# The skip term of an SSM on GpSimd, and one slot for each kind of projection weights

## The chip, the cores and the metric

The kernel runs on one core of a Trainium2 chip. The metric is the device time of one execution, in microseconds (us). A core has a matrix engine (TensorE, PE in the profile), VectorE (DVE), ScalarE (ACT), GpSimd (POOL) and SyncE (SP). Each works through its own queue in order and waits for the others by semaphores. Here nearly all transfers are issued from SP's queue, in the order in which the program was written; if one of them has to wait, those behind it wait too. TensorE writes to PSUM, in eight banks of 128 x 512 f32; the other data is in SBUF.

## The reference

A state-space model (SSM) and an attention read the same x (2048 positions, 1024 features, bf16), and a gate mixes them for each position:

```
Bu   = x @ B_bar^T                      (complex, 1024 states)
h[t] = Lam_bar * h[t-1] + Bu[t]
a    = 2 * Re(h @ C^T) + x * Dskip
b    = softmax(q k^T / sqrt(32)) v @ wo     (32 heads of 32, q k v = x @ wqkv)
g    = sigmoid(sum(x * gate_w))
out  = g * a + (1 - g) * b
```

The change is in how `x * Dskip`, the skip term, gets into `g * a`.

## The kernel before

**Bursts.** The backbone is 512 bursts: 8 groups of 4 heads, 8 blocks of 256 queries in a group, 8 steps over the keys in a block. A burst (function `burst`, line 1612) issues eight score matmuls (L1624) into four PSUM banks, and two exponentials of 1024 columns on ACT (L1643). Three pairs of banks take turns, so the scores of a burst wait until the first exponential of the burst before is over. In 184 bursts DVE computes a quarter of the second exponential by a polynomial: one operation takes the scores out of PSUM (L1633), and ACT's shortened exponential (L1640, 768 columns) is ordered behind it; then three passes on DVE (L1667, L1668, L1664), and one on GpSimd (L1665, into the tile xp) for each pair of such bursts. TensorE multiplies the exponentials by V (L1709, and L1688 for those from xp). At the end of a block DVE normalizes (L1722, L1723), and a transposing transfer stores the result.

**Dense work.** All other matmuls are cut into chains that are laid between the bursts, four matmuls of 512 columns (or as many columns) to a burst. All chains of the loop in `build` (line 1734) accumulate in bank 7, one after the other, and each ends with an eviction by DVE:

- u chains (`d_u`, L1457, eviction L1461): x times B, 64 of them; the result goes to DRAM and comes back as items (load L1474), for which DVE does the rotation and the scan (`item_ops`, L1353 and L1362). The weights B come through a ring of three slots (L1076).
- projection chains (`d_qk` L1426, `d_v` L1445): K, V and Q of the next group, 12 for each group.
- C chains (`d_c`, line 1496): 32, each for 128 positions and 512 features: 16 matmuls of h with C (L1504), and four matmuls of 128 columns (L1510) with x and a diagonal matrix of Dskip, which add x * Dskip into the same bank. The eviction (L1517) multiplies by the gate into one f32 tile (Ag), and the tile is stored to DRAM (L1518).
- output chains (`d_out`, L1535): attention output times wo; their eviction (L1547) adds g * a, loaded again (L1527).

**Order.** `build` writes the program burst by burst, and picks the next chain by fixed rules: projections when the group's end comes near, else C chains, else u chains. A C chain may begin when the items of its chunk are done and C has been folded (`fold_ops`, 24 operations of DVE, queued when the last of C has been asked for). It counts a chain's weight in matmuls of 512 columns; the four small matmuls of a C chain have weight 0. From estimated times it decides between which chains the operations of DVE are put. In the 496 bursts of the loop there is dense work in every one, the last 4 with one matmul only.

**Memory.** K and V weights have two slots (groups in turn), Q weights one: `wq`, `wkv`. `ld_w` (line 1068) loads 256 KB; K and V of group g + 2 are asked for at burst 25 of group g, Q of group g + 1 at burst 28. C comes in 8 pairs of transposing loads (L1081), one pair every four bursts from burst 28 (`C_LOADS`). In the early bursts the tiles for C still hold exponentials (`plan`). wo comes in parts: rows 0 and 1 at burst 386 into slots of K and V, the rest after the last C chain, row 7 behind the last projection.

Of the kernel before, what the change touches and what calls it, by code (L numbers as in the profile page):

```python
# [6 lines left out]
BF = mybir.dt.bfloat16  # L7
# [925 lines left out]
C_LOADS = 28  # L933
# [25 lines left out]
class FastPath:  # L959

    def __init__(self, nc, S, es, d, flag):
# [17 lines left out]
        self.wo3 = [row(1024, 2), row(5120, 3), row(3072, 1), self.cT[0][:, 0:1, :], self.cT[0][:, 1:2, :]]  # L979
        self.wo = [(self.wo3[0][:, a, :], "wo0") for a in range(2)] + [(self.wo3[4][:, 0, :], "wo4")] + [(self.wo3[1][:, a, :], "wo1") for a in range(3)]  # L980
        self.wo += [(self.wo3[3][:, 0, :], "wo3"), (self.wo3[2][:, 0, :], "wo2")]
# [5 lines left out]
        self.hpx = wb[:, 5120:8192].rearrange("p (k n) -> p k n", k=6)  # L987
# [18 lines left out]
        self.diagD = T("diagD", [128, 8, 128], BF)  # L1006
# [58 lines left out]
    def w_of(self, g, part):  # L1065
        return (self.wkv[:, g % 2, part - 1], ("w", g % 2, part)) if part else (self.wq, ("w", 0, 0))
# [86 lines left out]
    def opening(self):  # L1153
# [10 lines left out]
        for word in self.OPENING.split():  # L1164
# [44 lines left out]
            elif op == "M":  # L1209
# [7 lines left out]
                self.diag_d()  # L1217
# [86 lines left out]
    def diag_d(self):  # L1304
        for j in range(8):
            self.pool(lambda e, j=j: e.tensor_scalar(self.diagD[:, j, :], self.ident[:], self.pf[:, 3, j:j + 1], 0.0, ALU.mult, ALU.add),
                      ["ident", ("pf", 3)], [("diagD", j)])
# [188 lines left out]
    def d_c(self, ch, tq, cb, k):  # L1496
# [11 lines left out]
        for q in range(4):  # L1508
            dt = 4 * cb + q
            mms.insert(5 * q + 3, (0, lambda e, f, l, q=q, dt=dt: e.matmul(ps[:, 7, 128 * q:128 * (q + 1)], xT[:, dt, 128 * tt:128 * (tt + 1)], self.diagD[:, dt, :],  # L1510
                                                                          start=False, stop=False), [("diagD", dt)] + self.xtok(ch)))
        a = self.Ag
        at = "Ag"
        tile = 2 * tt + cb

        def evac():
            self.dve(lambda e: e.tensor_scalar(a, ps[:, 7, :], self.gcol[:, 0, tt:tt + 1], None, ALU.mult), [("bank", 7), "g0"], [at], "evac_c")  # L1517
# [3 lines left out]
        return self.chain(mms, "c", evac)  # L1521
# [212 lines left out]
    def build(self):  # L1734
# [10 lines left out]
        for part in (1, 2):  # L1745
            self.ld_w(1, part)
# [38 lines left out]
        wo1 = wo6 = last = False  # L1785
# [4 lines left out]
        for p in range(first, NBURST):  # L1790
# [41 lines left out]
            if pg == 25 and g + 2 < GROUPS:  # L1832
                assert g or not (proj[0] or cur and cur.tag == "proj")
                for part in (1, 2):
                    self.ld_w(g + 2, part)
            if pg == 28 and g + 1 < GROUPS:
                assert not (cur and cur.tag == "proj")
# [4 lines left out]
            if not cs and cur is None and not wo1 and self.c_left[3] == 0:  # L1842
# [293 lines left out]
```

## Time and profile before

| | us |
|---|---|
| three runs | 927.49, 926.35, 927.41 |
| median | 927.41 |
| profiled execution | 928.11 |
| its span, first to last instruction | 926.3 |
| ACT busy | 907.3 |
| PE busy | 902.5 |
| DVE busy | 758.4 |
| POOL busy | 86.8 |

A row of a group reads: line, engine, operation, output <- inputs, shapes and count | busy time in us, mean in ns of one | idle time of the engine just ahead of them, and who ended it. A row of the timeline reads: start, duration, line, operation, and in brackets the idle time ahead of it with its releaser. PE's times include the depth of the array: matmuls overlap, so the distance of two starts says more than a duration. The same holds for ACT's exponentials, which start a little before the one ahead has drained. SPq rows are the issue of a transfer, not the transfer.

### The profile page before, as it was taken

The numbers are of one execution on the slowest core, as the hardware profiler recorded it, in microseconds if no ns is written. First come the engines' busy times: TensorE is split into PE (matmuls) and PEld (weight loads), VectorE is DVE, ScalarE is ACT, GpSimd is POOL, SyncE is SP. The second block draws the span as 40 slices with busy tenths as digits, with TensorE's granted clock in tenths as the row PEclk, the third lists the DMA queues.
The fourth block names the chain that finished last, engine by engine and source line by source line (L and its number), as shares of the span: only waits on it lengthen the run. The fifth ranks groups of instructions, "written<-read, shape, count | busy, mean of one in ns | idle before, by whom it ended". The sixth has DMA issues, their size and how long they took to land.

```text
span 926.3 us, 33979 instructions
## 1 busy us (share of the span) xinstructions
PE 902.5 (97%) x15316; PEld 503.9 (54%) x15316; DVE 758.4 (82%) x1310; ACT 907.3 (98%) x1034; POOL 86.8 (9%) x156
## 2 busy tenths in 40 slices
PE   8899999999999999999999999999999999999996
PEld 4554754557555565546655565555655655445553
DVE  2788989998989999989989999899988655776665
ACT  6999999999999999999999999999999999999996
POOL 2000000111000101011111020000010010001010
PEclk9999999999999999999999999999999999999998
DMA  9569747750457101272012511413001112424312
GB/s 195 87 116 184 93 84 138 144 116 5 81 113 152 50 20 49 67 147 53 19 51 65 126 45 31 104 63 103 20 15 43 31 51 77 156 83 128 114 62 75
DMA packets 170934, 77.69 MB, mean 84 GB/s; under 512 B 147232, under 2 KB 155424, under 8 KB 170784
## 3 DMA queue, kind: packets, MB, share of 16 engines
q1 hardware_dynamic: 168624, 74.94, 36.3%
q8 instruction: 121, 1.98, 0.9%
q10 hardware_dynamic: 2160, 0.53, 0.3%
q14 instruction: 29, 0.24, 0.1%
HBM read 25.18 MB, written 20.97 MB: 50 GB/s over the span
## 4 chain that ended last, share of the span: by engine, by line
PE 52%; ACT 40%; DVE 4%; DMA 2%; SPq 1%; issue 1%; POOL 0%; DVEq 0%; ACTq 0%
ACT f_pt L1643 32%; PE f_ps L1709 14%; PE f_ps L1624 10%; PE f_ps L1426 9%; PE f_ps L1504 7%; PE f_ps L1457 6%; ACT f_pt L1640 5%; PE f_ps L1445 5%; SPq L1062 1%; ACT f_cT L1643 1%; PE f_ps L1688 1%; DMA f_xT<-in_A_x_dram 1%; ACT f_Et L1643 1%; DMA f_wb<-in_A_B_im_dram 1%; DMA f_ub<-u_scratch 0%
## 5 line engine op out<-in xcount | busy, mean ns | idle before, releaser
L1643 ACT ACTIVATE f_pt<-f_ps 128x1024 bf16<-128x1024 f32 x760 | 728.8, 1090 | 1.5 <-PE f_ps L1624 1.3
L1709 PEld LDWEIGHTS f_ps<-f_V,f_pt 128*128 128x128 bf16 x7184 | 222.2, 96 | 95.3 <-issue 68.7
L1709 PE MATMUL f_ps<-f_V,f_pt 128*128 128x33 bf16 x7184 | 258.0, 178 | 0.0
L1624 PE MATMUL f_ps<-f_Q,f_K 32*128 32x256 bf16 x4096 | 203.3, 273 | 10.8 <-ACT f_pt L1643 3.3
L1640 ACT ACTIVATE f_pt<-f_ps 128x768 bf16<-128x768 f32 x184 | 165.3, 898 | 0.7 <-PE f_ps L1624 0.6
L1624 PEld LDWEIGHTS f_ps<-f_Q,f_K 32*128 32x128 bf16 x4096 | 60.7, 92 | 148.0 <-ACT f_pt L1643 120.6
L1457 PE MATMUL f_ps<-f_xT,f_wb 128*128 128x512 bf16 x512 | 131.5, 379 | 1.6 <-DMA f_wb<-in_A_B_im_dram 0.7
L1665 POOL TENSOR_SCALAR f_xp<-f_xq 128x512 int16<-128x512 f32 x92 | 67.3, 732 | 646.0 <-DVE f_xq L1664 471.3
L1426 PE MATMUL f_ps<-f_xT,f_wb 128*128 128x512 bf16 x464 | 119.3, 379 | 0.1
L1633 DVE TENSOR_SCALAR f_xi<-f_ps 128x256 int32<-128x256 f32 x184 | 77.4, 421 | 17.6 <-PE f_ps L1624 13.3
L1362 DVE TENSOR_TENSOR_SCAN f_ht<-f_pf,f_init,f_ut 128x512 bf16<-128x512 f32 x64 | 81.3, 1279 | 0.0
L1504 PE MATMUL f_ps<-f_cT,f_hp 128*128 128x512 bf16 x272 | 74.5, 379 | 0.1
L1667 DVE SCALAR_TENSOR_TENSOR f_xq<-f_xi 128x512 f32<-128x512 uint16 x92 | 63.7, 692 | 3.2
L1668 DVE SCALAR_TENSOR_TENSOR f_xq<-f_xq,f_xi 128x512 f32<-128x512 f32 x92 | 63.6, 692 | 3.1
L1664 DVE SCALAR_TENSOR_TENSOR f_xq<-f_xi,f_xq 128x512 f32<-128x512 int16 x92 | 63.5, 690 | 2.6
L1457 PEld LDWEIGHTS f_ps<-f_xT,f_wb 128*128 128x128 bf16 x512 | 40.1, 96 | 40.5 <-issue 8.6
L1535 PE MATMUL f_ps<-f_wb,f_OT 128*128 128x512 bf16 x188 | 61.2, 381 | 0.4 <-DVE f_Et L1547 0.4
L1445 PE MATMUL f_ps<-f_wb,f_xT 128*128 128x128 bf16 x896 | 59.3, 219 | 0.0
L1426 PEld LDWEIGHTS f_ps<-f_xT,f_wb 128*128 128x128 bf16 x464 | 36.1, 96 | 35.6 <-issue 7.6
L1461 DVE CAST f_ub<-f_ps 128x512 bf16<-128x512 f32 x64 | 44.1, 688 | 10.4 <-PE f_ps L1457 9.7
L1445 PEld LDWEIGHTS f_ps<-f_wb,f_xT 128*128 128x128 bf16 x896 | 50.4, 97 | 3.8 <-issue 3.8
L1722 DVE RECIPROCAL f_rc<-f_ps 128x8 f32<-128x8 f32 x63 | 13.1, 207 | 47.6 <-PE f_ps L1688 43.5
(149 smaller groups left out, 822.5 us busy)
## 6 DMA issues: line engine op xcount, KB each, us to landing
u_scratch<-f_ub SPq DMA_DIRECT2D x64, 128.0 KB, 2.1
f_ub<-u_scratch SPq DMA_DIRECT2D x32, 256.0 KB, 3.0
ag_scratch<-f_Ag SPq DMA_DIRECT2D x32, 256.0 KB, 2.0
f_hp<-ag_scratch SPq DMA_DIRECT2D x32, 256.0 KB, 3.0
f_wb<-in_B_wqkv_dram SPq DMA_DIRECT2D x21, 256.0 KB, 4.1
out_dram<-f_xT SPq DMA_DIRECT2D x16, 256.0 KB, 2.2
f_OT<-f_On SPq DMA_TRANSPOSE x63, 2.3
f_wb<-in_B_wo_dram SPq DMA_DIRECT2D x1, 768.0 KB
```

Of the source, the lines that this page charges most:

```text
L1362: ops.append((1.24, lambda ri=ri: dve(lambda e: e.tensor_tensor_scan(ht[:, ri, :], rr, ut[:, ri, :], self.init[:, ri, j:j + 1], ALU.mult, ...
L1426: mms.append((1, lambda e, f, l, a=a, w=w: e.matmul(ps[:, bank, :], w[:, a, :], xT[:, a, 512 * ch:512 * (ch + 1)], start=f, stop=l), [tok] ...
L1445: m = e.matmul(ps[:, bank, 128 * q:128 * (q + 1)], xT[:, a, 128 * kt:128 * (kt + 1)], w[:, a, :], start=(a == 0), stop=(a == 7))
L1457: mms.append((1, lambda e, f, l, a=a: e.matmul(ps[:, 7, :], bT[:, (2 * n + ri) % 3, a, :], xT[:, a, 512 * ch:512 * (ch + 1)], start=f, sto ...
L1504: mms.append((1, lambda e, f, l, j=j, ri=ri, h=h: e.matmul(ps[:, 7, :], h[:, cols], cT[ri][:, j, 512 * cb:512 * (cb + 1)], start=f, stop=l ...
L1624: m = e.matmul(ps[:, 2 * sl[h // 2] + h % 2, 256 * kl:256 * (kl + 1)], K[32 * h:32 * h + 32, g % 2, 128 * kt:128 * (kt + 1)], Q[32 * h:32 ...
L1633: first = self.dve(lambda e: e.tensor_scalar(self.xi[:, b % 2, X_COLS * n:X_COLS * (n + 1)], ps[:, 2 * s + 1, 512 - X_COLS:512], X_A, X_LO ...
L1640: self.S.op("act", lambda e: e.activation(flat(self.tile[p]), flat(ps[:, 2 * s:2 * s + 2, :]), ACT.Exp, scale=SCALE), reads=[("S", s)], wr ...
L1643: self.act(lambda e: e.activation(self.tile[p], ps[:, 2 * s:2 * s + 2, :], ACT.Exp, scale=SCALE), [("S", s)], [("pt", p)], "exp")
L1665: self.pool(lambda e: e.tensor_scalar(bits, xq[:], X_K, 128.0 * (E0 + 126.0), ALU.mult, ALU.add), ["xq"], p2, "x_p")
L1667: return [(0.73, 0.0, lambda: self.dve(lambda e: e.scalar_tensor_tensor(xq[:], lo, E2 / E3 * w, lo, ALU.add, ALU.mult), i2, ["xq"], "x_q") ...
L1709: m = e.matmul(ps[:, 6, o:o + 33], self.tile[p][:, h2, 256 * kl + 128 * qt:256 * kl + 128 * (qt + 1)], V[:, g % 2, 2 * i + kl, h, :], star ...
```

## The change

1. The diagonal matrices (`diag_d`, eight operations of GpSimd) and the four small matmuls in each C chain go.
2. In their place GpSimd computes, for each C chain, x times Dskip times the gate into an f32 tile: a product of a piece of x (rows of x as they lie in DRAM, 128 x 512 bf16, loaded for it into one of two slots, `ld_skip`) with Dskip spread over all partitions (`Dbc`, one load at burst 70), and a scaling by the gate (`skip`). Both are written into the program where the chain begins; the next chain's piece of x is asked for two bursts later. There are two f32 tiles in place of one.
3. The eviction multiplies the bank by the gate and adds that tile, in one operation; the store follows as before.
4. Q's, K's and V's weights have one slot each. K and V of group g + 1 are loaded at burst 0 of group g, Q at burst 38 (`W_AT`); for group 1, V comes at the start and K at burst 17. A K chain may not begin ahead of burst 4, nor a Q chain ahead of burst 42.
5. C's loads begin at burst 32 in place of 28; the folding follows them.
6. Output weights: seven rows, one load each, behind the last C chain (into the freed tiles of C and the ring of B), row 7 later as before.

```diff
-C_LOADS = 28
+C_LOADS = 32
+W_AT = (38, 0, 17)
...
-        wb = T("wb", [128, 8192], BF)
-        self.wq = wb[:, 0:1024].rearrange("p (a n) -> p a n", a=8)
-        self.wkv = wb[:, 1024:5120].rearrange("p (s q a n) -> p s q a n", s=2, q=2, a=8)
-        self.bT = wb[:, 5120:8192].rearrange("p (s a n) -> p s a n", s=3, a=8)
+        wb = T("wb", [128, 6144], BF)
+        self.wqkv = [wb[:, 1024 * k:1024 * (k + 1)].rearrange("p (a n) -> p a n", a=8) for k in range(3)]
+        self.bT = wb[:, 3072:6144].rearrange("p (s a n) -> p s a n", s=3, a=8)
...
-        self.diagD = T("diagD", [128, 8, 128], BF)
+        self.Dbc = T("Dbc", [128, 1024], BF)
+        self.xn = T("xn", [128, 2, 512], BF)
+        self.Agt = [self.Ag, T("A2", [128, 512], F32)[:]]
...
+    def ld_skip(self, dn):
+        tt, cb = divmod(dn.tile, 2)
+        k = dn.k
+        self.dma(lambda e: e.dma_start(self.xn[:, k], self.x2[128 * tt:128 * (tt + 1), 512 * cb:512 * (cb + 1)]), [], [("xn", k)], "ld_xn")
+
+    def skip(self, dn):
+        tt, cb = divmod(dn.tile, 2)
+        k = dn.k
+        a, at = self.Agt[k], ("Ag", k)
+        self.pool(lambda e: e.tensor_tensor(a, self.xn[:, k], self.Dbc[:, 512 * cb:512 * (cb + 1)], ALU.mult), [("xn", k), "Dbc"], [at], "skip")
+        self.pool(lambda e: e.tensor_scalar(a, a, self.gcol[:, 0, tt:tt + 1], 0.0, ALU.mult, ALU.add), ["g0"], [at], "skip")
...
-        for q in range(4):
-            dt = 4 * cb + q
-            mms.insert(5 * q + 3, (0, lambda e, f, l, q=q, dt=dt: e.matmul(ps[:, 7, 128 * q:128 * (q + 1)], xT[:, dt, 128 * tt:128 * (tt + 1)], self.diagD[:, dt, :],
-                                                                          start=False, stop=False), [("diagD", dt)] + self.xtok(ch)))
...
-            self.dve(lambda e: e.tensor_scalar(a, ps[:, 7, :], self.gcol[:, 0, tt:tt + 1], None, ALU.mult), [("bank", 7), "g0"], [at], "evac_c")
+            a, at = self.Agt[k % 2], ("Ag", k % 2)
+            self.dve(lambda e: e.scalar_tensor_tensor(a, ps[:, 7, :], self.gcol[:, 0, tt:tt + 1], a, ALU.mult, ALU.add), [("bank", 7), "g0"], [at], "evac_c")
...
-        for part in (1, 2):
-            self.ld_w(1, part)
+        self.ld_w(1, 2)
...
-                proj[g][8 + c].after = max(16 * c, 32)
+                proj[g][c].after = W_AT[1] + 4
+                proj[g][8 + c].after = max(16 * c, W_AT[0] + 4)
...
+            if p == 70:
+                self.dma(lambda e: e.dma_start(self.Dbc[:], self.d["A_Dskip"].unsqueeze(0).to_broadcast([128, 1024])), [], ["Dbc"], "ld_D")
+                self.ld_skip(cs[0][1])
...
-            if pg == 25 and g + 2 < GROUPS:
-                for part in (1, 2):
-                    self.ld_w(g + 2, part)
-            if pg == 28 and g + 1 < GROUPS:
+            if pg == W_AT[1 if g else 2] and g + 1 < GROUPS:
+                self.ld_w(g + 1, 1)
+                if g:
+                    self.ld_w(g + 1, 2)
+            if pg == W_AT[0] and g + 1 < GROUPS:
                 self.ld_w(g + 1, 0)
...
-            if p == 386:
-                self.dma(lambda e: e.dma_start(self.wo3[0], wsv[:, 0:2, :]), [], ["wo0"] + [("w", 0, q) for q in (1, 2)], "ld_wo")
...
+                for a in range(7):
+                    j = a if a < 3 else a - 3
+                    x = [("cT", 0, j), ("cTf", 0, j, 0), ("cTf", 0, j, 1)]
+                    if a in (3, 4, 5):
+                        x = [("bT", a - 3)] + [("hp", 8, k) for k in (2 * a - 6, 2 * a - 5)]
+                    self.dma(lambda e, a=a: e.dma_start(self.wo[a][0], wsv[:, a, :]), [], ["wo%d" % a] + x, "ld_wo")
...
                             cur = cs.pop(0)[1]
+                            self.skip(cur)
+                            if cs:
+                                self.later.append((p + 2, lambda dn=cs[0][1]: self.ld_skip(dn)))
```

More of the change, by code (lines that the diff above doesn't have):

```diff
@@ L1065, in w_of @@
     def w_of(self, g, part):
-        return (self.wkv[:, g % 2, part - 1], ("w", g % 2, part)) if part else (self.wq, ("w", 0, 0))
+        return self.wqkv[part], ("w", 0, part)
     def ld_w(self, g, part, eng="sp"):
@@ L1520, in evac @@
             self.c_end = self.p
-        return self.chain(mms, "c", evac)
+        dn = self.chain(mms, "c", evac)
+        dn.tile, dn.k = tile, k % 2
+        return dn
     def ld_a(self, k):
@@ L1784, in build @@
         first = FIRST
-        wo1 = wo6 = last = False
+        wo1 = last = False
         nal = nc = 0
@@ L1838, in build @@
+            if pg == W_AT[0] and g + 1 < GROUPS:
+                assert not proj[0]
                 self.ld_w(g + 1, 0)
             wsv = self.d["B_wo"].rearrange("(a p) n -> p a n", p=128)
[L1840 to L1842 removed]
+            if not wo1 and not cs and cur is None and self.c_left[3] == 0:
@@ L1849, in build @@
             if g >= 6 and not last and not proj[7] and not us and not cs and cur is None and not self.bg:
                 last = True
-                xs = [("xr", r) for r in range(16)]
-                assert wo1 and wo6
-                self.dma(lambda e: e.dma_start(self.wo3[2], wsv[:, 7:8, :]), [], ["wo2"] + [("w", 1, q) for q in (1, 2)] + xs, "ld_wo")
+                assert wo1
+                self.dma(lambda e: e.dma_start(self.wo[7][0], wsv[:, 7, :]), [], ["wo7", ("cT", 0, 4), ("cTf", 0, 4, 0), ("cTf", 0, 4, 1)], "ld_wo")
@@ L2002, in tail @@
                 S.op("pe", lambda e, r=r, cb=cb, bank=bank: e.matmul(ps[:, bank, :], OT[:, 7, 1792 + 128 * r:1920 + 128 * r], wo[7][0][:, 512 * cb:512 * (cb + 1)],
-                                                                    start=(cb == 1), stop=True), reads=[("OT", 7, 7, r), "wo2"], name="tail", **w)
+                                                                    start=(cb == 1), stop=True), reads=[("OT", 7, 7, r), "wo7"], name="tail", **w)
             if r == 0:
```

22 lines of the change are left out of this document (4 added, 18 removed).

## The prediction

> **What bounds the kernel now.** I read the head of the page first (busy shares, then the chain that ended last), then ScalarE's busy time stage by stage, then the list of waits.
>
> ```profile
> span 926.3 us, 33979 instructions
> PE 902.5 (97%) x15316; PEld 503.9 (54%) x15316; DVE 758.4 (82%) x1310; ACT 907.3 (98%) x1034; POOL 86.8 (9%) x156
> PE 52%; ACT 40%; DVE 4%; DMA 2%; SPq 1%; issue 1%; POOL 0%; DVEq 0%; ACTq 0%
> ```
>
> Two engines look full, and the chain runs through both, so the page alone does not say which one a relief of TensorE would help. The stage table does. Its columns are the stretch, its length, and the busy time of PE, PE's weight loads, DVE, ACT and POOL. The first three rows hold the head, the largest hole between head and tail, and the tail; the other five are the stretches in which the SSM output chains (the C chains) run.
>
> ```profile
> 0.00:25.00 25.00, 20.14 (x209) 11.65 (x209) 6.71 (x22) 16.46 (x21) 4.85 (x22) 1.00 1.05 197
> ...
> 75.00:100.00 25.00, 24.71 (x486) 14.95 (x487) 23.22 (x33) 23.66 (x27) 0.19 (x1) 1.00 0.94 152
> ...
> 900.00:925.00 25.00, 18.07 (x284) 9.07 (x282) 14.47 (x45) 19.03 (x24) 1.24 (x2) 0.87 0.20 68
> ```
>
> ```profile
> 295.00:310.00 15.00, 14.87 (x257) 8.03 (x252) 13.90 (x23) 15.00 (x18) 1.70 (x2) 1.00 0.55 121
> 351.00:394.00 43.00, 42.99 (x719) 23.10 (x715) 39.50 (x65) 43.00 (x50) 4.21 (x6) 1.00 0.20 62
> 460.00:517.00 57.00, 56.71 (x930) 30.66 (x928) 51.40 (x84) 56.66 (x65) 6.11 (x10) 1.00 0.18 53
> 602.00:645.00 43.00, 42.98 (x715) 23.28 (x712) 39.85 (x65) 43.00 (x49) 3.66 (x5) 1.00 0.27 77
> 724.00:781.00 57.00, 57.00 (x953) 30.61 (x954) 32.09 (x57) 56.87 (x66) 4.94 (x8) 1.00 0.14 44
> ```
>
> ACT is idle for 926.3 - 907.3 = 19.0 us, of which the first 25 us hold 8.5 and the stretch from 900 holds 6.0 plus what follows 925 (up to 1.3); 1.34 lie at 75 to 100, and about 2 are scattered. In the C stretches its idle time sums to 0 + 0 + 0.34 + 0 + 0.13 = 0.47 us. ACT, with the exponentials, is the bound there. The list of waits (who waited for whom: us, times, longest) says the same from the other side: TensorE's score matmuls wait for ACT.
>
> ```profile
> PEld f_ps L1624 <- ACT f_pt L1643: 120.6, 312, 1.0
> ...
> DVE f_Ag L1517 <- PE f_ps L1504: 13.1, 18, 2.3
> ```
>
> So TensorE waits 0.39 us in each of 312 of the 512 bursts. A kernel bound this way gives little for TensorE time taken away; what can hurt is anything that makes ACT or TensorE wait for DVE, which in the first four C stretches is busy 92% of the time (144.65 of 158 us).
>
> **1. TensorE loses 128 small matmuls.** Four diagonal matmuls per C chain, 32 chains. Timeline of one:
>
> ```profile
> 300.48 0.22 PE L1510 MATMUL f_ps<-f_diagD,f_xT 128*128 128x128 bf16 x1
> ...
> 300.54 0.38 PE L1504 MATMUL f_ps<-f_cT,f_hp 128*128 128x512 bf16 x1
> ...
> 300.85 0.12 PEld L1624 LDWEIGHTS f_ps<-f_Q,f_K 32*128 32x128 bf16 x8 [0.26 <-ACT f_pt L1643]
> ```
>
> The next matmul starts 0.06 us after the diagonal one, so it costs 0.06, not its 0.22; 128 x 0.06 = 7.7 us of TensorE. Right behind it, the next burst's scores wait 0.26 us for ACT: in such bursts the relief only lengthens that wait. Ends: 0 and -7.7. ACT's idle time in these stretches is the nearest row (0.47), but overlapping exponentials hide short waits in a busy share; I take -1.0.
>
> **2. Eviction and GpSimd.** Eight small GpSimd operations at the start go; nobody was held by them: nothing. The eviction changes its form.
>
> ```profile
> L1517 DVE TENSOR_SCALAR f_Ag<-f_ps,f_gcol 128x512 f32<-128x512 f32 x32 | 23.8, 744 | 13.4 <-PE f_ps L1504 13.1
> ...
> L1547 DVE SCALAR_TENSOR_TENSOR f_Et<-f_ps,f_gcol,f_hp 128x512 f32<-128x512 f32 x4 | 3.0, 747 | 2.1 <-PE f_ps L1535 2.1
> ```
>
> 32 x 0.003 = +0.1 us of DVE: nothing. New on GpSimd are 32 products of two bf16 tiles and 32 scalings of an f32 tile, 128x512 each. The scaling is like the last step of the DVE exponential (L1665). It shows what these do to DVE; first beside an eviction, then beside a scan, then between two products:
>
> ```profile
> 365.07 0.62 POOL L1665 TENSOR_SCALAR f_xp<-f_xq 128x512 int16<-128x512 f32 x1 [2.84 <-DVE f_xq L1664]
> 365.16 0.75 DVE L1517 TENSOR_SCALAR f_Ag<-f_ps,f_gcol 128x512 f32<-128x512 f32 x1 [0.17 <-PE f_ps L1504]
> ...
> 395.03 1.27 DVE L1362 TENSOR_TENSOR_SCAN f_ht<-f_pf,f_init,f_ut 128x512 bf16<-128x512 f32 x1
> 395.20 1.52 POOL L1665 TENSOR_SCALAR f_xp<-f_xq 128x512 int16<-128x512 f32 x1 [9.75 <-DVE f_xq L1664]
> ...
> 492.14 0.69 DVE L1353 TENSOR_TENSOR f_ht<-f_ub,f_Et 128x1024 bf16<-128x1024 bf16 x1
> 492.31 0.99 POOL L1665 TENSOR_SCALAR f_xp<-f_xq 128x512 int16<-128x512 f32 x1 [4.99 <-DVE f_xq L1664]
> 492.74 1.10 DVE L1353 TENSOR_TENSOR f_tq<-f_ub,f_Et 128x1024 bf16<-128x1024 bf16 x1
> ```
>
> Beside an eviction, which reads PSUM, both keep their times (0.62, 0.75). Beside operations with two SBUF tensors GpSimd waits for the running one (0.62 becomes 1.52 or 0.99), and the next one of DVE waits for GpSimd: 1.10 for 0.69, +0.41 us. That is the price of a scaling, where DVE has such work without a gap. The product is not in the trace at this size: between 0.41 (no dearer than the scaling) and 1.03 us (twice the scaling's 0.62, less the 0.21 that did not block).
>
> How often? In the stretch 460 to 517, first the products and sums of the items (L1353), then the scans (L1362), DVE time alone:
>
> ```profile
> 460.00:517.00 57.00, 19.99 (x33) 1.00 0.18 53
> ...
> 460.00:517.00 57.00, 10.11 (x8) 1.00 0.18 53
> ```
>
> 30.1 of 57 us, a share of 0.53 (a lower figure, the three passes of the DVE exponential come on top). Of the chains, 22 lie in the first four stretches; the last stretch has DVE idle for 25 us and costs nothing. Added DVE time: 22 x 0.53 x (0.41 + 0.41) = 9.6 us up to 22 x 0.53 x (0.41 + 1.03) = 16.8. DVE's idle time there is 158 - 144.65 = 13.4 us. If all of it could absorb, 0 to 3.4 are left; if none, 9.6 to 16.8. Lateness is absorbed only where an idle spot comes before the next operation that someone waits for, and these are close together: the DVE share of an exponential (ACT's second exponential of the burst waits for it), the eviction (the next chain needs its bank), the normalization. I take +5.0, above the 3.4 and well under half of the added upper figure, since the largest idle spots, 13.1 us before 18 evictions, lie at the end of a chain, behind the DVE exponentials and not ahead of them. Ends 0 and +16.8.
>
> [...]
>
> **3. New waits.** The product waits for its piece of x (128 KB) and for the store of the chain two before. Behind it on GpSimd stand the last steps of DVE exponentials, for which TensorE waits. The load goes out two bursts (2 x 926.3/512 = 3.6 us) before the chain, and can go earlier, for it stands behind no wait but those of the SP queue (the item loads and stores).
>
> ```profile
> ag_scratch<-f_Ag SPq DMA_DIRECT2D x32, 256.0 KB, 2.0
> f_wb<-in_B_wqkv_dram SPq DMA_DIRECT2D x21, 256.0 KB, 4.1
> ```
>
> At under 2.0 us for a 256 KB transfer it lands in time, and the store is over long before: 0. Without this cover each late piece holds GpSimd, and the eviction has still 4 bursts (7.2 us).
>
> **4. Weights in one slot.** K and V of a group are now loaded at its predecessor's first burst. In most groups the first use is 30 bursts later. In the seventh it is only 4 (7.2 us) later, against 4.1 to land: hidden by 3 us; uncovered it would cost its lateness once. Q moves from burst 28 to 38, with first use from 52: nothing.
>
> **5. Output weights.** 512 KB that were loaded at burst 386 now come with the rest behind the last C chain.
>
> ```profile
> 780.00:798.00 18.00, 17.97 (x324) 10.35 (x322) 13.04 (x23) 17.98 (x22) 1.82 (x3) 1.00 0.64 214
> L1535 PE MATMUL f_ps<-f_wb,f_OT x188: 376/379/592, 798.3 to 915.3; 128*128 128x512 bf16 x188
> ```
>
> The first output matmul is at 798.3, 18 us on, with the DMA engines at 0.64 and 214 GB/s (3.85 MB). Another 0.5 MB makes about 0.73: hidden, 0.
>
> **6. C later, Q weights away from the C loads.** This touches the hole at 77 us:
>
> ```profile
> 66.79 1.30 SPq L1081 DMA_TRANSPOSE f_cT<-in_A_C_im_dram  x1
> 68.14 1.28 SPq L1071 DMA_DIRECT2D f_wb<-in_B_wqkv_dram  x1
> 69.53 0.67 SPq L1474 DMA_DIRECT2D f_ub<-u_scratch  x1
> ...
> 73.34 0.69 DVE L1353 TENSOR_TENSOR f_ht<-f_ub,f_Et 128x1024 bf16<-128x1024 bf16 x1 [2.39 <-DMA f_ub<-u_scratch]
> ...
> 77.36 1.94 ACT L1643 ACTIVATE f_OT<-f_ps 128x1024 bf16<-128x1024 f32 x2 [1.34 <-PE f_ps L1624]
> ```
>
> The SP queue is full with C loads and the Q weights, so an item's load leaves late, DVE waits 2.39 us for it, a normalization stands behind that wait, TensorE behind the normalization, and ACT is idle 1.34 us. After the change neither the Q weights (1.28 us of SP) nor a C load stands at this burst, so this hole closes; what is late next is the item load four bursts on, beside the first C loads. Ends: -1.34 (gone), +1.34 (a second hole of its size). I take -1.0, since projections, which ask SP for nothing, begin at burst 36.
>
> **The sum.** 928.11 (the profiled execution: span 926.3 and 1.8 around it) - 1.0 (part 1) + 5.0 (part 2) - 1.0 (part 6) + 0 (parts 3 to 5) = 931.1. The profiled execution stands 0.7 us above the median of the three runs (927.41), so 930.4 on the median's scale, +0.3%.
>
> **The rivals.**
>
> *GpSimd's work falls into gaps* (the other side). Place: the first four C stretches. Against it: the 1.10 us row. For it: GpSimd may start as soon as its inputs are there, mid-chain, and 0.47 of DVE's time is open to it; the 13.4 us of idle exceed the 9.6 of the lower added figure. It decides when less than 0.15 us of lateness reaches ACT: then 927.4 - 2.0 = 925.4, and with all of ACT's scattered idle gone (19.0 - 8.5 - 6.0 - 1.3 = 3.2) 924.2. I put it at 925.0.
>
> *Gain and loss cancel.* Between 0.15 and 3.9 us of lateness: 925.6 to 929.3, middle 927.4. For it: TensorE's waits of 0.39 us can take up a late eviction. Against it: ACT's own wait for the DVE exponential has no such cushion.
>
> *DVE is blocked for all of each GpSimd operation.* If the full 0.62 and 1.24 us count and not the blocked part alone, the added time is 22 x 0.53 x 1.86 = 21.7 us; less all idle, 8.3; so 927.4 - 2.0 + 8.3 = 933.7 at least and 947.1 at most, 937 where nearly a half of the idle absorbs. Against it: in the row at 492 DVE lost 0.41 and not 0.62. [...]
>
> *Weights late in their one slot.* K of the last group, if SP is held more than 3 us at burst 384: TensorE stands still for the rest, say 3 us, 928.4 without part 2 and 933.4 with it. The row of landings (4.1 in the median) speaks against it.
>
> **How the numbers follow.** The forecast (929.3 to 934.5 as its own range) has 0.43, full blocking 0.12, late weights 0.03: slower together 0.58. Cancelling has 0.22: 0.2%, 1.85 us, is about what a measurement of this kernel can tell from no change. Gaps have 0.20. The range goes from 925.0, the gap rival, to 938, past the middle of the full-blocking one; outside it lie half of the gap rival and half of the full-blocking one, and little else.
>
> **What would show it.** ACT's idle time in the four C stretches: 0.3 us before, some 5 after. The DVE operations of L1353 with a maximum well over 1.1 us, and evictions that no longer wait for TensorE (13.1 us before 18 of them now). GpSimd busy for some 50 us more. The product's duration on GpSimd: 0.6 to 1.2 us where it is undisturbed. TensorE's waits for ACT in the C stretches longer by 0.06 a burst, if ACT stays the bound. ACT's hole at 77 us gone. I am wrong if the C stretches keep their length (then GpSimd's work is hidden, and the time falls), or if the loss comes from elsewhere: a hole at bursts 384 to 388, one at the output chains' start, or one among the C loads.

## The result, and the profile after

| us | median | lowest to highest | runs |
|---|---|---|---|
| before | 926.88 | 926.05 to 928.04 | 6 |
| after | 937.62 | 933.54 to 939.8 | 6 |

The kernel became slower: a ratio of 1.011, interval 1.0087 to 1.0133, or +10.7 us. The forecast was +3. Direction and mechanism were right, the size was not. The range, 925.0 to 938, holds the median with 0.4 us to spare, and two of the six executions of after lie above it. Its upper end was taken from a rival (GpSimd blocks DVE for the whole of its operations) whose mechanism the runs do not bear out, so that the range held is luck. The profiled execution of after took 938.45 us.

The head of its page (span, busy shares, the chain that ended last):

```profile
span 936.6 us, 33826 instructions
PE 901.7 (96%) x15188; PEld 493.5 (53%) x15188; DVE 775.8 (83%) x1310; ACT 908.4 (97%) x1034; POOL 159.3 (17%) x212
PE 49%; ACT 34%; DVE 11%; issue 2%; SPq 1%; DMA 1%; POOL 1%; DVEq 0%; ACTq 0%
```

DVE runs the same 1310 instructions and is busy for 17.4 us more (758.4 before). Its share of the last chain went from 4% to 11%. ACT's busy time grew by 1.1 us alone, so some 9 of the 10.3 us by which the span grew are idle time of ACT.

Where it lies is read from the stage table of after. The rows are the same five stretches of SSM chains, cut at the same exponentials of ACT as in the prediction; the columns are stretch, length, busy time of PE, weight loads, DVE, ACT, POOL, and then the granted clock.

```profile
293.43:308.35 14.92, 14.66 (x250) 7.23 (x246) 13.88 (x23) 14.92 (x18) 4.26 (x4) 1.00 0.33 88
349.44:396.90 47.46, 43.80 (x695) 21.23 (x691) 44.15 (x67) 43.69 (x50) 15.88 (x17) 0.96 0.29 84
462.44:524.13 61.69, 55.98 (x898) 28.02 (x896) 57.43 (x84) 57.59 (x65) 26.19 (x26) 1.00 0.25 71
608.99:656.48 47.49, 43.99 (x693) 21.68 (x690) 44.43 (x65) 43.68 (x49) 19.07 (x17) 0.96 0.22 70
735.35:791.26 55.91, 55.73 (x923) 27.67 (x924) 32.15 (x58) 55.91 (x66) 17.91 (x22) 1.00 0.20 61
```

The first four were 158 us long and are 171.6 now. ACT is idle in them for 171.6 - 159.9 = 11.7 us, where it was 0.34. All of the growth lies in the second to the fourth. The fifth, in which DVE has time to spare, is 1.1 us shorter. (The prediction has every SSM chain in these five stretches; two of the 32 run between the fourth and the fifth, and no time was lost there.) Two rows have a granted clock of 0.96; more of that below.

The list of waits of after (who waited for whom: us, times, longest):

```profile
DVE f_Ag L1520 <- PE f_ps L1512: 9.5, 7, 2.2
...
ACT f_pt L1648 <- PE f_ps L1629: 7.0, 14, 1.3
PEld f_ps L1512 <- DVE f_Ag L1520: 6.8, 6, 1.6
PE f_ps L1512 <- DVE f_Ag L1520: 6.2, 6, 1.5
...
ACT f_pt L1645 <- DVE f_xi L1638: 5.2, 8, 0.9
```

L1520 is the eviction of an SSM chain, L1512 its matmuls, L1638 the DVE share of an exponential, and L1645 and L1648 are the exponentials on ACT. An eviction in the four stretches used to be on time; now the next chain waits for it, up to 1.5 us. The last row is the bare form of the loss: ACT waits for DVE. All of its 5.2 us lie in the four stretches. Of the 7.0 us for which ACT waits for scores, 6.2 lie there: 2.9 in or just behind the halved clock (below), 1.5 behind two late steps of GpSimd (see part 3), and six waits of 0.30, each behind a shortened exponential. Together that is 11.4 of ACT's 11.7 us.

One such place, in the timeline of after (start, duration, then the idle time ahead in brackets):

```profile
376.78 1.36 POOL L1314 TENSOR_TENSOR f_Ag<-f_xn,f_Dbc 128x512 f32<-128x512 bf16 x1 [0.66 <-DMA f_xn<-in_A_x_dram]
...
377.05 1.38 DVE L1361 TENSOR_TENSOR f_OT<-f_ut,f_tq 128x512 bf16<-128x512 bf16 x1
...
378.24 0.75 POOL L1315 TENSOR_SCALAR f_Ag<-f_Ag,f_gcol 128x512 f32<-128x512 f32 x1
378.35 0.41 DVE L1638 TENSOR_SCALAR f_xi<-f_ps 128x256 int32<-128x256 f32 x1
...
378.80 0.81 ACT L1645 ACTIVATE f_pt<-f_ps 128x768 bf16<-128x768 f32 x1 [0.73 <-DVE f_xi L1638]
...
380.57 0.40 PE L1629 MATMUL f_ps<-f_Q,f_K 32*128 32x256 bf16 x8 [0.70 <-ACT f_pt L1648]
...
382.18 1.84 PE L1512 MATMUL f_ps<-f_cT,f_hp 128*128 128x512 bf16 x4 [0.76 <-DVE f_A L1520]
...
384.61 1.94 ACT L1648 ACTIVATE f_pt<-f_ps 128x1024 bf16<-128x1024 f32 x2 [1.34 <-PE f_ps L1629]
...
387.01 1.02 PE L1512 MATMUL f_ps<-f_cT,f_hp 128*128 128x512 bf16 x4
```

GpSimd's product starts at 376.78. The item's last sum on DVE starts at 377.05 and takes 1.38 us, where its median is 0.42: DVE lost 0.96. The DVE share of the exponential stands behind it, and ACT idles 0.73 us. The eviction is late too, TensorE idles 0.76, and then four matmuls take 1.84 us, where four of the same form take 1.02 at 387. The granted clock says why:

```profile
379.00:382.00 3.00, 1.72 (x41) 1.08 (x38) 2.96 (x5) 3.00 (x4) 0.00 (x0) 1.00 0.02 5
382.00:385.00 3.00, 2.82 (x29) 1.06 (x30) 3.00 (x5) 1.66 (x3) 0.99 (x1) 0.54 0.67 198
385.00:388.00 3.00, 3.00 (x41) 1.20 (x41) 1.82 (x3) 2.84 (x4) 0.00 (x0) 0.89 0.07 20
```

Right behind the wait, TensorE's clock is halved for 3.41 us (382.26 to 385.67, by the trace's records of the granted clock), and ACT waits 1.34 us for scores. The same happens at 648.50, behind a wait of 1.49 us:

```profile
648.35 1.78 PE L1512 MATMUL f_ps<-f_cT,f_hp 128*128 128x512 bf16 x4 [1.49 <-DVE f_Ag L1520]
```

The profile of before has no such stretch ahead of its last 12 us.

### The profile page after: what moved, and what is told of

It is laid out like the page before. It is cut to its first block, busy times and chain, and to the rows that moved or that the text cites. A ratio compares the mean times of both kernels' runs of the same rounds, so it can differ in the third digit from the quotient of the medians.

```text
span 936.6 us, 33826 instructions
## 1 busy us (share of the span) xinstructions
PE 901.7 (96%) x15188; PEld 493.5 (53%) x15188; DVE 775.8 (83%) x1310; ACT 908.4 (97%) x1034; POOL 159.3 (17%) x212
## 4 chain that ended last, share of the span: by engine, by line
PE 49%; ACT 34%; DVE 11%; issue 2%; SPq 1%; DMA 1%; POOL 1%; DVEq 0%; ACTq 0%
ACT f_pt L1648 27%; PE f_ps L1714 12%; PE f_ps L1629 10%; PE f_ps L1434 9%; PE f_ps L1465 6%; PE f_ps L1512 6%; ACT f_pt L1645 5%; PE f_ps L1453 5%; DVE f_ht L1370 1%; DVE f_ut L1361 1%; SPq L1064 1%; DVE f_tq L1361 1%; ACT f_cT L1648 1%; DVE f_xq L1672 1%; PE f_ps L1693 1%
## 5 line engine op out<-in xcount | busy, mean ns | idle before, releaser
L1648 ACT ACTIVATE f_pt<-f_ps 128x1024 bf16<-128x1024 f32 x760 | 730.5, 1094 | 7.3 <-PE f_ps L1629 7.0
L1645 ACT ACTIVATE f_pt<-f_ps 128x768 bf16<-128x768 f32 x184 | 165.2, 898 | 5.9 <-DVE f_xi L1638 5.2
L1629 PEld LDWEIGHTS f_ps<-f_Q,f_K 32*128 32x128 bf16 x4096 | 60.8, 92 | 171.3 <-ACT f_pt L1648 141.0
L1638 DVE TENSOR_SCALAR f_xi<-f_ps 128x256 int32<-128x256 f32 x184 | 77.3, 420 | 14.7 <-PE f_ps L1629 10.2
L1370 DVE TENSOR_TENSOR_SCAN f_ht<-f_pf,f_init,f_ut 128x512 bf16<-128x512 f32 x64 | 86.3, 1357 | 0.0
L1512 PE MATMUL f_ps<-f_cT,f_hp 128*128 128x512 bf16 x272 | 72.9, 389 | 4.8 <-DVE f_Ag L1520 3.2
L1673 DVE SCALAR_TENSOR_TENSOR f_xq<-f_xq,f_xi 128x512 f32<-128x512 f32 x92 | 65.6, 713 | 3.1
L1540 PE MATMUL f_ps<-f_cT,f_OT 128*128 128x512 bf16 x156 | 45.0, 380 | 0.4 <-DVE f_Et L1552 0.4
```

Of the source, the lines that this page charges most:

```text
L1370: ops.append((1.24, lambda ri=ri: dve(lambda e: e.tensor_tensor_scan(ht[:, ri, :], rr, ut[:, ri, :], self.init[:, ri, j:j + 1], ALU.mult, ...
L1512: mms.append((1, lambda e, f, l, j=j, ri=ri, h=h: e.matmul(ps[:, 7, :], h[:, cols], cT[ri][:, j, 512 * cb:512 * (cb + 1)], start=f, stop=l ...
L1629: m = e.matmul(ps[:, 2 * sl[h // 2] + h % 2, 256 * kl:256 * (kl + 1)], K[32 * h:32 * h + 32, g % 2, 128 * kt:128 * (kt + 1)], Q[32 * h:32 ...
L1638: first = self.dve(lambda e: e.tensor_scalar(self.xi[:, b % 2, X_COLS * n:X_COLS * (n + 1)], ps[:, 2 * s + 1, 512 - X_COLS:512], X_A, X_LO ...
L1645: self.S.op("act", lambda e: e.activation(flat(self.tile[p]), flat(ps[:, 2 * s:2 * s + 2, :]), ACT.Exp, scale=SCALE), reads=[("S", s)], wr ...
L1648: self.act(lambda e: e.activation(self.tile[p], ps[:, 2 * s:2 * s + 2, :], ACT.Exp, scale=SCALE), [("S", s)], [("pt", p)], "exp")
```

## The experiments

The ratio compares each with the kernel before on the same chip, whose median was 929.95 (runs 1, 3, 4 and 5), 928.61 (runs 2, 6, 8 and 10) or 928.24 (runs 7 and 9). On why these medians differ, see part 6 below. "Span" is that of the profiled execution; it was 926.3 before and 936.6 after.

**1. Everything but the skip term.** The diagonal matmuls come back, the loads of x go; weights, output weights and C as in the changed kernel.

```diff
-            self.dve(lambda e: e.scalar_tensor_tensor(a, ps[:, 7, :], self.gcol[:, 0, tt:tt + 1], a, ALU.mult, ALU.add), [("bank", 7), "g0"], [at], "evac_c")
+            self.dve(lambda e: e.tensor_scalar(a, ps[:, 7, :], self.gcol[:, 0, tt:tt + 1], None, ALU.mult), [("bank", 7), "g0"], [at], "evac_c")
...
-                            self.skip(cur)
...
+        for q in range(4):
+            dt = 4 * cb + q
+            mms.insert(5 * q + 3, (0, lambda e, f, l, q=q, dt=dt: e.matmul(ps[:, 7, 128 * q:128 * (q + 1)], xT[:, dt, 128 * tt:128 * (tt + 1)], self.diagD[:, dt, :],
+                                                                          start=False, stop=False), [("diagD", dt)] + self.xtok(ch)))
```

> The changed kernel with the skip term back on TensorE (diagonal matrices, four small matmuls in a C chain, eviction without the added tile, no pieces of x, no GpSimd work); weight slots, C loads and output weights stay as changed. Contention theory (GpSimd's two operations block DVE, all else is free or gains): 925 us, 2 below the kernel before, with the hole of ACT at 77 us gone. Rival (the weights' one slot, C later or the output weights cost the time): 933 or more.

925.72 us, ratio 0.9958 (0.9937 to 0.9978), span 923.9, as expected. Parts 4 to 6 together gain; the loss is in the skip term.

**2. C later, alone.** The kernel before with one number changed.

```diff
-C_LOADS = 28
+C_LOADS = 32
```

> The kernel before with the C loads from burst 32 in place of 28, nothing else. Theory (the hole at 77 us came from SP's queue, full with C loads and Q weights in front of an item load): the hole of 1.34 us goes, 1.3 us less in all. Rival (the Q weights at burst 28 alone made it): the hole stays.

926.37 us, ratio 0.9976 (0.9954 to 0.9997), span 923.1. It gains more than the 1.3 us that had been expected (2.2 by the medians, 3.2 by the spans), and in the profile as much as all of parts 4 to 6 together: the weight slots and output weights neither gain nor cost anything that these runs can tell. The stage table of this run has no hole of ACT left:

```profile
75.00:100.00 25.00, 24.69 (x506) 15.65 (x507) 23.20 (x32) 25.00 (x28) 0.38 (x2) 1.00 0.91 155
```

**3. The diagonals gone, nothing on GpSimd.** The loads of x stay; the skip term is missing.

```diff
-            self.dve(lambda e: e.scalar_tensor_tensor(a, ps[:, 7, :], self.gcol[:, 0, tt:tt + 1], a, ALU.mult, ALU.add), [("bank", 7), "g0"], [at], "evac_c")
+            self.dve(lambda e: e.tensor_scalar(a, ps[:, 7, :], self.gcol[:, 0, tt:tt + 1], None, ALU.mult), [("bank", 7), "g0"], [at], "evac_c")
...
-                            self.skip(cur)
```

> The changed kernel without GpSimd's two operations; the pieces of x are still loaded, the eviction is that of before, so x * Dskip is missing from the output. Contention theory: 924 us, 1 below the kernel with the diagonal back, for TensorE is relieved. Rival (32 more loads on SP's queue and the layout cost the time): 935 or more.

924.07 us, ratio 0.9929 (0.9906 to 0.9952), span 921.5. Against the run with the diagonals, 1.65 us less by the medians: that is what TensorE's relief is worth. In the profiles it is 2.4 us by the spans, of which 1.2 lie in the fifth stretch.

**4 and 5. The product without the scaling, and the scaling without the product.** In the first the gate is missing on the skip term; in the second the tiles are zeroed once, and the skip term is missing.

```diff
-        self.pool(lambda e: e.tensor_scalar(a, a, self.gcol[:, 0, tt:tt + 1], 0.0, ALU.mult, ALU.add), ["g0"], [at], "skip")
```

```diff
-        self.pool(lambda e: e.tensor_tensor(a, self.xn[:, k], self.Dbc[:, 512 * cb:512 * (cb + 1)], ALU.mult), [("xn", k), "Dbc"], [at], "skip")
```

> The changed kernel without the scaling by the gate on GpSimd, so the skip term is added ungated; one GpSimd operation in a chain, the product. Contention theory: the product holds about 1.0 of the 1.4 us that both hold, and lateness grows faster than in proportion: 930 to 933 us. Rival (the eviction waits for GpSimd's result, or GpSimd's queue is late for the exponentials): the wait stays with the product, 936.

> The changed kernel with the scaling alone, no product: the f32 tile is scaled in place, so x * Dskip is missing from the output; it still waits for the piece of x. Contention theory: 0.41 us held in a chain, less than DVE's idle time of 0.6: 925 to 927 us. Rival (the waits for the piece of x and for the store cost the time, whatever the work): 935.

Product alone: 929.19 us, ratio 0.9988 (0.9975 to 1.0001), span 928.3. Scaling alone: 924.25 us, ratio 0.9933 (0.9909 to 0.9956), span 922.1. Above the run with neither, the product costs 5.1 us and the scaling 0.2. Together they cost over 13 (next run). So the prices do not add. Both times lie a little under what had been expected.

**6. The changed kernel again,** on the chip of runs 2, 8 and 10.

> The changed kernel unchanged, on the chip of this group. Both theories: 1.1% above the kernel before. Contention theory with halved clock as its amplifier: its executions differ by 1.6 us for each 3.4 us stretch at half the TensorE clock (0.0018 of the granted clock). Rival (the lateness alone makes the loss): times and granted clocks do not go together.

937.24 us, ratio 1.0083 (1.0057 to 1.0109), span 935.6, with one stretch of half clock, not two. Times and granted clocks go together, as the contention theory had it: over the eleven executions of after, here and in the result, from 933.54 us at 0.997 to 939.8 at 0.990, a line through them gives 1.25 us for each 0.0018.

**7. Two scalings, no product.** Is it the product, with its two inputs, that does harm, or the time for which DVE is blocked? The tiles are zeroed once, and the skip term is missing.

```diff
-        self.pool(lambda e: e.tensor_tensor(a, self.xn[:, k], self.Dbc[:, 512 * cb:512 * (cb + 1)], ALU.mult), [("xn", k), "Dbc"], [at], "skip")
+        self.pool(lambda e: e.tensor_scalar(a, a, self.gcol[:, 0, tt:tt + 1], 0.0, ALU.mult, ALU.add), ["g0", ("xn", k)], [at], "skip")
         self.pool(lambda e: e.tensor_scalar(a, a, self.gcol[:, 0, tt:tt + 1], 0.0, ALU.mult, ALU.add), ["g0", ("xn", k)], [at], "skip")
```

> The kernel with GpSimd's work but without its product: the tile is filled with zeros once, and GpSimd runs the scaling twice for each SSM chain, one after the other (the skip term is missing from the result). One scaling for a chain gave 924.25, one product alone 929.19, both 937.4. If what counts is the time for which DVE is blocked in each chain, whoever blocks it, two scalings block 2 x 0.41 = 0.82 us, nearly as much as one product (0.96), and the time comes to 926 to 929.5. If only the product, with its two SBUF inputs, does harm, a second scaling is as free as the first: 924.0 to 925.0.

928.51 us, ratio 1.0001 (0.9991 to 1.0011). The second scaling costs 4.3 us by the medians (on two chips), 5.2 by the spans and 0.0068 of 928 = 6.3 by the ratios; the first cost 0.2. So a second scaling is not free: the blocked time counts, whichever operation blocks. The pages of this run, of the product alone and of the run with neither:

```profile
span 927.3 us, 33607 instructions
...
PE 878.5 (95%) x14967; PEld 492.7 (53%) x15188; DVE 767.3 (83%) x1310; ACT 907.1 (98%) x1034; POOL 145.8 (16%) x214
```

```profile
span 928.3 us, 33573 instructions
...
PE 878.5 (95%) x14967; PEld 492.7 (53%) x15188; DVE 769.6 (83%) x1310; ACT 907.2 (98%) x1034; POOL 123.9 (13%) x180
```

```profile
span 921.5 us, 33527 instructions
...
PE 878.8 (95%) x14967; PEld 492.1 (53%) x15188; DVE 757.8 (82%) x1310; ACT 905.7 (98%) x1034; POOL 84.9 (9%) x148
```

DVE's busy time is a good first measure. All of these kernels give DVE 1310 operations with the same shapes, so what it is busy beyond 757.8 us is time for which GpSimd blocked it (and 0.1 for the eviction's other form):

| GpSimd's work for a chain | DVE busy above 757.8 | span above 921.5 | not passed on |
|---|---|---|---|
| one scaling | 3.7 | 0.6 | 3.1 |
| two scalings | 9.5 | 5.8 | 3.7 |
| product | 11.8 | 6.8 | 5.0 |
| both (run 6) | 18.2 | 14.1 | 4.1 |
| both (first profile of after) | 18.0 | 15.1 | 2.9 |
| both, product held back (run 8) | 19.0 | 10.4 | 8.6 |

In the first five rows 3 to 5 us of DVE's added time are absorbed, and the rest goes through. In the fourth and fifth row about 1.6 and 3.2 us of the span are the halved clock (an estimate from the last section); without these, 12.5 and 11.9 are passed on, and some 6 absorbed. The last row shows that the amount alone does not settle it: where in the chain DVE is blocked counts too.

**8. The product held back until TensorE is through with the chain before,** so that it runs beside that chain's eviction, which reads PSUM.

```diff
-        self.pool(lambda e: e.tensor_tensor(a, self.xn[:, k], self.Dbc[:, 512 * cb:512 * (cb + 1)], ALU.mult), [("xn", k), "Dbc"], [at], "skip")
+        last = [o for o in self.S.q["pe"] if o.name == "c"][-1:]
+        self.S.op("pool", lambda e: e.tensor_tensor(a, self.xn[:, k], self.Dbc[:, 512 * cb:512 * (cb + 1)], ALU.mult), reads=[("xn", k), "Dbc"], writes=[at], deps=last, name="skip")
```

> The changed kernel with one wait more: the product of a chain waits for the last matmul of the chain before, so it runs while DVE evicts from PSUM (0.75 us without a second SBUF tensor) and only its rest and the scaling meet DVE's two-tensor work. Contention theory: a good half of the loss goes, 929 to 932 us on the scale of 926.9 for the kernel before. Rival (the eviction and the exponentials wait for late GpSimd results): starting later makes it worse, 938 or more.

934.26 us, ratio 1.0055 (1.0036 to 1.0074), span 931.9, DVE busy 776.8. A miss: a good half of the loss was to go, and 3.0 of 8.6 us went. DVE is blocked as long as in run 6 (19.0 us above 757.8, against 18.2). What went is the stretch of half clock, and some of ACT's waits for DVE; of the 3.7 us between the spans of the two runs, 3.0 lie in the fourth stretch, where run 6 has its halved clock. Its waits:

```profile
PE f_ps L1513 <- DVE f_Ag L1521: 5.3, 6, 1.4
...
ACT f_pt L1646 <- DVE f_xi L1639: 2.8, 5, 1.0
```

So the place of a product within a chain is worth some 3 us. A product takes 1.15 us undisturbed and an eviction 0.75, so the eviction can cover little of a product and a scaling.

**9. Late evictions without GpSimd.** The kernel before, with four evictions repeated.

```diff
+HOLD = {4: 1, 10: 2, 16: 3, 20: 4}
...
-            self.dve(lambda e: e.tensor_scalar(a, ps[:, 7, :], self.gcol[:, 0, tt:tt + 1], None, ALU.mult), [("bank", 7), "g0"], [at], "evac_c")
+            for _ in range(1 + HOLD.get(tile, 0)):
+                self.dve(lambda e: e.tensor_scalar(a, ps[:, 7, :], self.gcol[:, 0, tt:tt + 1], None, ALU.mult), [("bank", 7), "g0"], [at], "evac_c")
```

> The kernel before, with the eviction of four SSM output chains of four different stretches repeated: once, twice, three and four times more, 0.75 us of DVE each, so that the next chain of TensorE starts up to 0.75, 1.5, 2.25 and 3.0 us later. No GpSimd work is added. If TensorE's clock halves because TensorE stood still for about a microsecond, the trace shows a granted clock of 0.5 for about 3.4 us behind the two or three longest of the four holds, and the time is 4 to 9 us above that of the kernel before (holds of 7.5 us in sum less what DVE's gaps and TensorE's waits absorb, plus about 1.6 for each halving). If the halving needs GpSimd's traffic, the clock stays at 1.00 behind all four, and the time is 0 to 5 us above.

938.93 us, ratio 1.0113 (1.0078 to 1.0147): 10.7 us for 7.5 us of added DVE time, more than either theory had. The span, 938.6, is 12.3 above before. TensorE's waits behind the four, and the stage rows beside the second, the third and the fourth of them:

```profile
361.92 0.59 PE L1505 MATMUL f_ps<-f_cT,f_hp 128*128 128x512 bf16 x2 [0.88 <-DVE f_Ag L1519]
...
479.90 0.59 PE L1505 MATMUL f_ps<-f_cT,f_OT 128*128 128x512 bf16 x2 [1.47 <-DVE f_Ag L1519]
...
616.39 1.06 PE L1505 MATMUL f_ps<-f_cT,f_hp 128*128 128x512 bf16 x2 [2.58 <-DVE f_xi L1635]
...
634.94 0.59 PE L1505 MATMUL f_ps<-f_cT,f_hp 128*128 128x512 bf16 x2 [3.39 <-DVE f_Ag L1519]
```

```profile
480.00:483.00 3.00, 3.00 (x50) 1.46 (x48) 2.87 (x6) 2.64 (x4) 0.00 (x0) 1.00 0.41 106
...
616.00:619.00 3.00, 2.61 (x25) 1.19 (x27) 0.86 (x2) 1.23 (x2) 0.62 (x1) 0.50 0.23 87
...
636.00:639.00 3.00, 3.00 (x38) 1.19 (x31) 2.48 (x7) 1.97 (x3) 0.00 (x0) 0.55 0.17 47
```

Behind 2.58 and 3.39 us the clock is halved, behind 0.88 and 1.47 it is not. GpSimd is not needed for it (its busy time is 0.00 in the 3.41 us ahead of each halving of this run, see the last section): in this run TensorE standing still was enough. Not all of the loss belongs to the holds. In the profile of this run the hole of ACT at 77 us, in code that is the kernel before's, is 3.09 us wide and not 1.34: there TensorE waits 1.63 and 0.70 us shortly after one another, and a third stretch of halved clock begins at 76.51.

```profile
78.69 1.94 ACT L1645 ACTIVATE f_OT<-f_ps 128x1024 bf16<-128x1024 f32 x2 [3.09 <-PE f_ps L1626]
```

Cut at the same exponentials, the profile is longer than that of before by 2.1 us around this hole, 0.7 behind the one extra eviction (0.75 us of DVE), 1.4 behind the two (1.5), and 8.1 in the stretch with the three and the four (5.25) and their two halvings. A late eviction is passed on nearly whole.

**10. GpSimd where DVE has room.** The diagonal matmuls for the first 24 chains, GpSimd for the last eight; Dskip is loaded over the diagonals when these are done with.

```diff
+        self.Dbc = self.diagD[:].rearrange("p a n -> p (a n)")
...
+        for q in range(4 if ch < 3 else 0):
...
+                            if cch == 3:
+                                self.skip(cur)
```

> The changed kernel with the skip term on TensorE for the first three chunks of positions (24 C chains) and on GpSimd for the last chunk (8 chains), where DVE is idle 44% of the time; Dskip is loaded over the diagonal matrices when these are done. Contention theory: all gains and no loss, 1.1 us below the kernel with the diagonal back, 923.5 to 924.5 on the scale of 926.9. Rival (GpSimd's work costs time wherever it stands): 925.5 or more, no better than with the diagonal everywhere.

924.34 us, ratio 0.9951 (0.9935 to 0.9967), span 923.1. It is faster than both kernels: 4.3 us under before on the same chip, and DVE is busy for 758.2 us, as before. Half of this by the medians is C's later loading (2.2 us, run 2), and all of it by the spans (both 923.1); against the run with all diagonals (0.9958) the difference is within the intervals.

## Why the prediction was right or wrong

**What bounds the kernel:** right. ACT's idle time in the four stretches was to go from 0.3 to some 5 us; it went to 11.7. Two of the waits are those that were named: ACT for the DVE exponential, the next chain for the eviction.

**Part 1, TensorE's relief, -1.0:** right; -1.65 by the medians. Of the 7.7 us of TensorE time that were reckoned to go, about a fifth arrived, since ACT was the bound.

**Part 2, GpSimd blocks DVE, +5.0:** this is the term that was mis-sized, at about a third of what was measured. By the spans GpSimd's work cost 15.1 us (936.6 against 921.5), by the medians 13.2 (937.24 against 924.07, on two chips). Two of its steps were sound. The scaling's block was taken from a row, and the product's hold was bounded by 0.41 and 1.03: DVE lost 0.96 to it. The product itself, undisturbed, takes this long:

```profile
388.54 1.15 POOL L1314 TENSOR_TENSOR f_A<-f_xn,f_Dbc 128x512 f32<-128x512 bf16 x1
```

It lies within the 0.6 to 1.2 us that were named for it. The added DVE time of the four stretches was put at 9.6 to 16.8 us; the rows show 159.9 - 144.7 = 15.2 (and 17.4 in the whole program; that ACT's busy time there is 159.9 too is chance). What failed is the step from added to passed-on time: +5.0 was "above the 3.4 and well under half of the added upper figure", because idle spots of DVE were thought to take up most of it. But the four stretches grew by 13.6 us for these 15.2, or by some 10 without the two halved stretches of clock. The sum of DVE's idle time, 13.4 us, was no measure of the cushion: it lies in pieces behind operations that somebody waits for, as the prediction itself said before it took the value.

The second thing that it lacked is the halved clock, which the sum has at nothing: some 1.3 to 1.6 us for each stretch (an estimate, see the last section), two in the profile of after and one in that of the repetition. Over the executions the granted clock varies, and the time with it (run 6).

**Part 3, new waits, 0:** too low by some 1.5 us. GpSimd does wait for its pieces of x, which land after a median of 2.7 us where under 2.0 had been reckoned, but it reaches the product early, and no operation of DVE waits for GpSimd in the list. Behind those products and scalings a last step of a DVE exponential came late twice, and ACT waited for scores behind both (1.12 and 0.36 us). The list of waits, and the first of the two places:

```profile
POOL f_A L1314 <- DMA f_xn<-in_A_x_dram: 27.5, 9, 4.8
...
PE f_ps L1693 <- POOL f_xp L1670: 1.9, 2, 1.4
```

```profile
473.72 0.27 PE L1693 MATMUL f_ps<-f_V,f_xp 128*128 128x33 bf16 x4 [1.38 <-POOL f_xp L1670]
...
475.24 1.02 ACT L1648 ACTIVATE f_pt<-f_ps 128x1024 bf16<-128x1024 f32 x1 [1.12 <-PE f_ps L1629]
```

TensorE's wait for GpSimd was 0.3 us before, once. It is 0.3 with one scaling, 1.2 with two, and 0.7 with the product alone, so it grows with GpSimd's added work. No run takes this wait away by itself; the table of run 7 has it in the passed-on time.

**Parts 4 and 5, 0:** right; the kernel before with C later alone does as well as all of the layout.

**Part 6, the hole at 77 us, -1.0:** right in mechanism, too small. The hole closed (ACT is busy for all of 75 to 100 us with C later alone), and C's later loading alone is worth 2.2 us by the medians and 3.2 by the spans. One profile showed a hole of 1.34 us; in another it is 3.09, with the clock halved in it. The executions of before differ in the same way: on the chip of runs 2, 6, 8 and 10 the median is 927.51 us for the seven with a granted clock of 0.997 or more and 930.94 for the five with 0.994 or less. That these have their halved clock at this hole is likely, but only one profile shows it. If so, the mean price of the hole is above what the first profile said, and the medians of before differ by how often it happened. Also the wait of ACT at 411 us (0.33 before) is gone, with C later alone too.

**The rivals.** The one with the nearest time, 937, had the wrong reason: it let DVE be blocked for all of each GpSimd operation and half of that be absorbed. Measured is the blocked part alone (15.2 us in the four stretches, not 21.7), and far less absorbed. Its sum also has a slip: for 937, 10.1 us have to be absorbed, which is nearly half of the added time but three quarters of the 13.4 us of idle time that the text names. Gaps and cancellation fell, except where GpSimd's work is a single scaling. Late weights were not seen.

**The other signs:** GpSimd is busy for 72.5 us more, where some 50 were expected: a product takes 1.24 us on average (1.15 undisturbed), and a scaling 1.11 where 0.62 had been reckoned, for what GpSimd waits for DVE within an operation counts as busy (the 1.52 us beside a scan, for 0.62, in the prediction's rows). The evictions still wait for TensorE, 10.8 us before 13 of them, where these waits were to go (13.1 before 18). TensorE's waits for ACT became 0.06 us longer on average in the whole program (141.0 us in 315), as forecast for the C stretches.

## What to carry to other kernels

Where a helper engine blocks an engine that is 92% busy, as here, count the blocked time of the busy one (its busy time in the profile, at the same instruction count, is a first measure) and take most of it as lost, beyond the first few us (13.6 us for 15.2 in the four stretches, some 10 without the halved clock); the sum of its idle time is no cushion. A small addition (3.7 us here) may pass for free and mislead about the next one of the same size: test at full dose. Put such work where the busy engine has room, as the last eight chains had (run 10: 924.34 us).

## What was not expected of the hardware

TensorE's granted clock falls to half in the middle of a dense program, each time for 3.41 us. The twelve profiles hold six such stretches ahead of the tail: at 382.26 and 648.50 us in after, at 647.98 in its repetition, and at 76.51, 615.82 and 636.30 in the run with late evictions.

The starts are not free. Within each profile they lie whole multiples of 3.4133 us apart, those in the tail among them (648.50 - 382.26 = 266.24 = 78 x 3.4133; 636.30 - 615.82 = 20.48 = 6 x 3.4133; 615.82 - 76.51 = 539.31 = 158 x 3.4133). So a profile can be cut on this grid, and the window ahead of each halved stretch looked at. The rows are: two windows of after, one of its repetition, five of the run with late evictions, and one of the run with the product alone. The first figure behind the length is TensorE's busy time.

```profile
378.85:382.26 3.41, 1.96 (x42) 1.27 (x41) 3.38 (x6) 3.41 (x5) 0.14 (x1) 1.00 0.02 5
645.09:648.50 3.41, 1.85 (x43) 1.25 (x42) 3.41 (x4) 2.65 (x3) 1.48 (x1) 1.00 0.00 0
...
644.57:647.98 3.41, 1.45 (x37) 1.02 (x34) 3.41 (x5) 2.32 (x4) 1.12 (x1) 1.00 0.00 0
...
73.10:76.51 3.41, 1.19 (x29) 0.80 (x30) 3.16 (x7) 2.51 (x3) 0.00 (x0) 1.00 1.24 146
475.87:479.28 3.41, 2.55 (x52) 1.52 (x51) 3.27 (x6) 3.08 (x4) 0.62 (x1) 1.00 0.03 5
612.41:615.82 3.41, 1.40 (x43) 1.05 (x41) 3.30 (x5) 2.09 (x3) 0.00 (x0) 1.00 0.00 0
629.48:632.89 3.41, 2.07 (x45) 1.37 (x43) 3.34 (x5) 2.93 (x4) 0.00 (x0) 1.00 0.23 71
632.89:636.30 3.41, 1.36 (x21) 0.76 (x23) 3.22 (x5) 0.92 (x2) 0.00 (x0) 1.00 0.20 77
...
377.58:380.99 3.41, 1.95 (x42) 1.29 (x42) 3.38 (x6) 3.41 (x5) 0.00 (x0) 1.00 0.02 5
```

The six windows with a halved stretch right behind them have TensorE busy for 1.19 to 1.96 of 3.41 us, so idle for 1.45 to 2.22. In every other window of the twelve profiles, from 30 us on to 15 us before the end, it is idle for at most 1.46 us (the last row; the next is 1.44), and the clock stays whole. In these profiles it is thus the idle time within one window of the grid that decides, at about 1.45 us, and not the length of one wait. At 382 in after, waits of 0.70 and 0.76 us add up. The wait of 1.47 us at 479.9 falls into two windows, with 0.86 us in the first, and has no effect. That of 3.39 us is split into 1.34 and 2.05, and the clock falls behind the second window alone. So the same wait may halve the clock in one execution and not in the next: after has a halved stretch at 382.26 us, its repetition none there.

At a granted clock of 0.50 a stretch takes at most half of its 3.41 us, 1.7, from TensorE. With the waits that go with it the runs of after give 1.3 to 1.6 us, an estimate: one stretch lowers the mean granted clock by 3.41 x 0.5 / 937 = 0.0018, a line through the eleven executions gives 1.25 us for that much, and the two ends of the first six (0.007 of the clock and 6.3 us apart, four stretches) give 1.6.
